# Two buffers instead of one for the rows of a tile that are scattered with gate and token

## The chip, the cores and the metric

The kernel runs on one core of a Trainium2 chip. The metric is the device time of one execution in microseconds (us).

The engines have these short names in the profile: PE is TensorE's matmul, PEld its weight load, DVE is VectorE, ACT is ScalarE, POOL is GpSimd and SP is SyncE, which issues most transfers. A "q" behind a name (SPq) is that engine's instruction queue.

## The reference

Three layers follow each other on 1152 tokens of 512 values.

```python
# attention: 2 batches, 8 heads, 576 positions, 64 values a head; each row keeps its 32 largest scores
scores = scale * q @ k.T
mask = scores >= kth_largest(scores, 32)
attn = softmax(where(mask, scores, -1e9)) @ v            # -> x [1152, 512]
# dense layer, 512 -> 2048 -> 512
h = x @ w_in
x = (h * cos(h)) @ w_out
# mixture of experts, 8 experts of width 1024, one expert per token
probs = softmax(x @ w_gate); e = argmax(x @ w_gate)
slot = place of the token among the tokens of expert e, in token order; kept if slot < 288
out[token] = probs[token, e] * (relu(x[token] @ w1[e]) @ w2[e])
```

## The kernel before

All operations are registered with a planner (`Plan`): engine, an estimated cost, the tiles that are read and written, and a rank. `Plan.emit` then simulates the engines with these costs. At each step it takes, over all engines, the operation that can start first, and among those of one engine that can start within 0.02 us of each other, the one of lowest rank (then the older in the list). So the order of instructions on each engine follows from these simulated times. A tile belongs to a ring with a fixed number of buffers; an operation that opens a new tile of a ring can be chosen only when a buffer is free in the simulation, and on the chip it waits by semaphore until the last user of the buffer is done.

There are 36 attention steps. The tokens form nine tiles of 128. The tiles are handled in groups: tile 0 alone, then the pairs (1, 2), (3, 4), (5, 6) and (7, 8). For each group the dense layer runs as `layer_in` (L662, matmuls L684 to L686), `cosine` (L712), `product` (L720, on GpSimd) and `layer_out` (L729), which sums a tile in the PSUM tile `x2` (two buffers). The matmuls of a pair's two tiles alternate, and those of the second end last.

Then each tile goes through `route` and `place`:

- `route`, L742: ScalarE copies `x2` into `xr`, a buffer of 128 rows of 520 values. L743 (helper line L660): TensorE transposes the rows into `pt` (two buffers). L744: ScalarE copies them to `gT` (one buffer). L748: four matmuls, recorded as eight instructions, give the logits in the PSUM tile `av` (one buffer, which logits and counts share). L751 to L756 (`pick`, VectorE) find the expert; L751 and L752 read `av`. L768: ScalarE takes the exponential. L759 to L761 write the gate into column 512 of `xr`; L764 and L765 (GpSimd) write the token number into column 513 and zeros behind it.
- `place`, L786: TensorE counts the earlier tokens of each expert, into `av`. L789 to L792 (`address`, VectorE) work out the slot of each row; L789 is the last that reads `av`. L795: GpSimd scatters the rows of `xr` to the DRAM tensor `xs` with an indirect transfer.

The buffer `xr` is in use from L742 until the scatter of L795 has landed. Tile 4 uses a buffer of its own, `xr4`, and its `place` comes last, after that of tile 8. The order in the list is route(7), place(7), route(8), place(8), place(4), at one rank for each pair.

When all nine scatters have landed, SyncE gathers the slots of expert 0 (L953, L956); transfers of later weights (L936, L939) stand behind it in the same queue. The experts follow: transposes (L963, L964), first layer (L978, L980), second layer (L1009), scatter to the output (L1015). Their weights are split into a high and a low part on ScalarE (L944) and VectorE (L946).

ScalarE changes its function table (ACT_TABLE_LOAD) whenever the sine of L712 and the exponentials of L561 and L768 alternate.

```python
    ring("x2", "ps", [128, 512], F32, 2)
    ring("av", "ps", [128, 512], F32, 1, tag="av")
    ring("gT", "mx", [128, 512], F32)
    ring("xr", "mx", [128, RW], F32)
    ring("xr4", "mx", [128, RW], F32, tag="raw")
    ...
        kx = ("xr4" if t == 4 else "xr", t)
```

Of the kernel before, what the change touches and what calls it, by code (L numbers as in the profile page):

```python
# [7 lines left out]
F32 = mybir.dt.float32  # L8
# [17 lines left out]
RW = 520  # L26
# [197 lines left out]
@with_exitstack  # L224
def kernel(ctx, tc, kq, vn, vs_, w_in, w_out, w_gate, w1, w2, capacity, out):

    assert int(capacity) == CAP
    ctx.enter_context(tc.manual_schedule())  # L230
    args = (tc, kq, vn, vs_, w_in, w_out, w_gate, w1, w2, out)
    const = ctx.enter_context(tc.tile_pool(name="const", bufs=1, side="left"))
    dram = ctx.enter_context(tc.tile_pool(name="dram", bufs=1, space=DRAM))
    kept = {}

    def lasting(name, shape, dtype, pool=const):
        if name not in kept:
            kept[name] = pool.tile(shape, dtype, name=name)
        return kept[name]
    kept["xs"] = dram.tile([SLOTS, RW], F32, name="xs")  # L240

    flag, more, unproven = forward(lasting, *args, True)
    with tc.If(flag() > 0):
        more()
        with tc.If(unproven() > 0):
            flag, more, _ = forward(lasting, *args, False)
            with tc.If(flag() > 0):
                more()
# [3 lines left out]
def forward(ctx, lasting, tc, kq, vn, vs_, w_in, w_out, w_gate, w1, w2, out, paired):  # L252
# [18 lines left out]
    def ring(name, pool, shape, dtype, bufs=1, tag=None, gate=None):  # L271
        P.ring(name, lambda: pools[pool], shape, dtype, bufs, tag, gate)
# [379 lines left out]
    ring("ur", "mx", [128, 2, 512], F32, 2, tag="ur")  # L652
    ring("nn", "mx", [128, 512], F32)
    ring("gT", "mx", [128, 512], F32)
    ring("xr", "mx", [128, RW], F32)
    ring("xr4", "mx", [128, RW], F32, tag="raw")

    def transposes(kp, src):
# [477 lines left out]
```

## Time and profile before

| | us |
|---|---|
| median of 3 runs | 705.67 (705.2 to 707.3) |
| profiled execution | 706.96 |
| its span (first to last instruction) | 705.1 |
| PE busy | 596.7 (85%) |
| PEld busy | 434.8 (62%) |
| DVE busy | 553.4 (78%) |
| ACT busy | 496.0 (70%) |
| POOL busy | 265.2 (38%) |

The share of busy time is a mean over stages that have different limits, so it doesn't tell by itself which engine bounds the kernel. All times within the span are counted from its first instruction. The granted clock of TensorE is given as a share of full speed: 1.00 is 2.4 GHz, 0.50 is 1.2 GHz, and a value between them is a stretch that has both.

### The profile page before, as it was taken

How to read it: one execution, taken by the hardware profiler on the slowest of the kernel's cores; microseconds unless marked ns; L12 is line 12 of the kernel's file. 1: busy time of each engine (PE TensorE's matmuls, PEld its weight loads, DVE VectorE, ACT ScalarE, POOL GpSimd, SP SyncE). 2: the span in 40 equal slices, each digit the busy share in tenths (PEclk: the TensorE clock that was granted, in tenths of full speed). 3: DMA queues.
4: the chain of work that ended last, by engine and by line, in shares of the span. 5: the costliest groups of instructions: out<-in, count | busy, mean ns of one | idle time of the engine just before them, and what ended most of it. 6: DMA issues, size and time to landing. Idle time of an engine off the chain costs nothing.

```text
span 705.1 us, 11071 instructions
## 1 busy us (share of the span) xinstructions
PE 596.7 (85%) x3611; PEld 434.8 (62%) x3611; DVE 553.4 (78%) x1654; ACT 496.0 (70%) x1004; POOL 265.2 (38%) x316
## 2 busy tenths in 40 slices
PE   3333576898999999989999899999639999999994
PEld 1122355645776655866665676666328888888893
DVE  5999999999999899999999953566115777779630
ACT  4666998999799988778877764476015777777630
POOL 3366675677345544554544432223110110011111
PEclk9999868999899999999999999999857999999998
DMA  8543552064221201100000003444023777778200
GB/s 330 198 150 122 164 163 91 1 236 172 67 89 39 76 0 38 35 1 17 1 1 1 1 17 119 140 144 150 31 78 119 230 241 223 226 257 254 71 17 16
DMA packets 29635, 76.24 MB, mean 108 GB/s; under 512 B 3966, under 2 KB 3966, under 8 KB 29568
## 3 DMA queue, kind: packets, MB, share of 16 engines
q1 hardware_dynamic: 27824, 70.68, 30.3%
q0 software_dynamic: 1744, 4.76, 1.8%
q8 instruction: 30, 0.49, 0.3%
q14 instruction: 37, 0.30, 0.2%
HBM read 63.52 MB, written 12.69 MB: 108 GB/s over the span
## 4 chain that ended last, share of the span: by engine, by line
PE 41%; DVE 34%; ACT 16%; DMA 3%; issue 3%; POOL 1%; SPq 1%; POOLq 0%; DVEq 0%; ACTq 0%
PE yp L1009 11%; DVE W L513 9%; DVE C L517 8%; PE hp L978 7%; PE x L729 7%; DVE C L509 4%; PE hp L980 3%; ACT Sp L561 2%; ACT pen L556 2%; DVE W L522 2%; DVE wt L405 2%; ACT Sp L570 2%; ACT Sp L494 2%; PE h L684 2%; DVE Sp L574 2%
## 5 line engine op out<-in xcount | busy, mean ns | idle before, releaser
L729 PE MATMUL x<-wo,hs 128*128 128x512 f32 x288 | 138.2, 603 | 0.0
L946 DVE TENSOR_TENSOR wl<-raw,wh 128x512 fp32r<-128x512 f32 x128 | 90.4, 741 | 41.9 <-ACT wh L944 38.7
L559 POOL TENSOR_TENSOR Sp<-Sp,pen 128x576 f32<-128x576 f32 x72 | 97.5, 1354 | 64.8 <-ACT pen L556 64.5
L513 DVE MAX8 W<-C 128x8 f32<-128x288 f32 x288 | 118.2, 446 | 0.6
L517 DVE MATCH_REPLACE8 C<-W,C 128x288 f32<-128x288 f32 x216 | 93.8, 440 | 0.0
L589 PE MATMUL pt<-ident,Sp 128*128 128x128 f32 x324 | 56.4, 304 | 38.6 <-ACT Sp L570 31.6
L482 PE MATMUL S<-kq 64*128 64x288 f32 x256 | 58.4, 539 | 30.8 <-ACT Sp L494 20.9
L944 ACT ACTIVATE wh<-raw 128x512 fp32r<-128x512 f32 x128 | 74.5, 622 | 9.9 <-DMA raw<-in_w_dram 6.9
L589 PEld LDWEIGHTS pt<-ident,Sp 128*128 128x128 f32 x324 | 40.4, 154 | 66.1 <-ACT Sp L570 41.0
L684 PE MATMUL h<-xh,wh 128*128 128x256 f32 x256 | 78.0, 305 | 0.5 <-ACT hs L691 0.4
L1015 POOL DMA_INDIRECT out_dram<-ot,ti x16 | 17.9, 1117 | 159.0 <-ACT ot L1024 124.8
L978 PE MATMUL hp<-xgs,wh 128*128 128x384 f32 x256 | 76.9, 370 | 0.0
L729 PEld LDWEIGHTS x<-wo,hs 128*128 128x128 f32 x288 | 49.0, 190 | 43.4 <-issue 42.7
L685 PE MATMUL h<-xl,wh 128*128 128x256 f32 x256 | 71.9, 281 | 0.0
L686 PE MATMUL h<-xh,wl 128*128 128x256 f32 x256 | 71.8, 281 | 0.0
L1009 PE MATMUL yp<-wh,hc 128*128 128x512 f32 x192 | 70.1, 405 | 0.0
L509 DVE TENSOR_TENSOR C<-Sp 128x576 f32<-128x576 f32 x72 | 64.5, 896 | 3.7 <-ACT Sp L494 2.9
L720 POOL TENSOR_TENSOR hs<-hs,ur 128x512 f32<-128x512 f32 x36 | 48.4, 1353 | 46.5 <-ACT ur L712 45.1
L980 PE MATMUL hp<-xgs,wl 128*128 128x192 f32 x256 | 65.5, 256 | 0.0
L561 ACT ACTIVATE Sp<-Sp,tb 128x576 f32<-128x576 f32 x72 | 55.7, 774 | 13.1 <-POOL Sp L559 12.9
L556 ACT ACTIVATE pen<-Sp,tb 128x576 bf16<-128x576 f32 x72 | 55.3, 768 | 6.3 <-POOL tb L549 5.5
L591 ACT ACTIVATE PT<-pt 128x384 f32<-128x384 f32 x108 | 48.5, 483 | 12.1 <-PE pt L589 12.0
(138 smaller groups left out, 1371.8 us busy)
## 6 DMA issues: line engine op xcount, KB each, us to landing
raw<-in_w_dram SPq DMA_DIRECT2D x64, 512.0 KB, 3.9
wraw<-in_w_out_dram SPq DMA_DIRECT2D x16, 512.0 KB, 3.9
wraw<-in_w_in_dram SPq DMA_DIRECT2D x16, 512.0 KB, 3.9
xs<-z SPq DMA_DIRECT2D x1, 4680.0 KB, 16.0
kq<-in_kq_dram SPq DMA_DIRECT2D x8, 576.0 KB, 7.8
v<-in_vn_dram SPq DMA_DIRECT2D x8, 320.0 KB, 5.5
v<-in_vs_dram SPq DMA_DIRECT2D x8, 320.0 KB, 3.0
out_dram<-z SPq DMA_DIRECT2D x1, 2304.0 KB, 21.0
```

Source lines behind the costliest of these rows:

```text
L509: DVE.tensor_tensor(out=T["C", s], in0=x[:, :, 0:HS], in1=x[:, :, HS:S], op=op)
L513: P.op("dve", 0.365, lambda r=r, i=i: DVE.max(T["W", s][:, i, LIST[r]:LIST[r] + 8], T["C", s][:, i, :]), r=[("C", s, i)], w=[("W", s, i)])
L517: P.op("dve", 0.42, lambda r=r, i=i: DVE.match_replace(T["C", s][:, i, :], T["W", s][:, i, LIST[r]:LIST[r] + 8], T["C", s][:, i, :], NEG), ...
L559: P.op("pool", 1.34, lambda i=i, kp=kp: POOL.tensor_tensor(out=T["Sp", s][:, i, :], in0=T["Sp", s][:, i, :], in1=T[kp], op=OP.subtract), r ...
L589: PE.transpose(T[kp][:, c * 128:(c + 1) * 128], P2[:, cc * 128:(cc + 1) * 128], ident)
L684: PE.matmul(o, hi, a, start=(kc == 0), stop=False, skip_group_check=True)
L729: P.op("pe", 0.86, lambda f=f, a=a: PE.matmul(T["x2", t], T[kh][:, a:a + 128], T["wo", 0][:, f, :], start=(f == 0), stop=(f == 15)), r=[kh ...
L944: P.op("act", 0.52, lambda a=a, hi=hi: ACT.activation(T[hi], T[kr][:, a * 512:(a + 1) * 512], AF.Copy), r=[kr], w=[hi])
L946: P.op("dve", 0.6, lambda a=a, hi=hi, lo=lo: DVE.tensor_tensor(out=T[lo], in0=T[kr][:, a * 512:(a + 1) * 512], in1=T[hi], op=OP.subtract), ...
L978: PE.matmul(T[kp][:, 0:2 * MAIN], T[ka][:, c:c + 128], x.rearrange("p a n -> p (a n)"), start=(kc == 0), stop=False, skip_group_check=True)
L980: PE.matmul(T[kp][:, 0:MAIN], T[kb][:, c:c + 128], x[:, 0], start=False, stop=(kc == 3), skip_group_check=True)
L1009: PE.matmul(T[kp], x, w, start=(fc + n == 0), stop=(fc == 7 and n == len(uses) - 1))
```

## The change

The ring `xr` gets two buffers. That is 2,080 bytes more in each partition of the pool `mx`. The planner's simulation counts with two buffers as well.

```diff
     ring("nn", "mx", [128, 512], F32)
     ring("gT", "mx", [128, 512], F32)
-    ring("xr", "mx", [128, RW], F32)
+    ring("xr", "mx", [128, RW], F32, 2)
     ring("xr4", "mx", [128, RW], F32, tag="raw")
```

## Rows read from the trace of the kernel before

**Rows 1.** Stretches: us, busy us (instructions) by engine, clock, DMA share, GB/s.
```profile
283.00:415.00 132.00, 124.91 (x891) 90.00 (x889) 127.28 (x421) 100.00 (x192) 64.63 (x84) 1.00 0.03 10
415.00:503.00 88.00, 87.98 (x455) 57.03 (x452) 38.93 (x84) 48.16 (x85) 22.42 (x23) 1.00 0.35 114
503.00:527.00 24.00, 6.68 (x61) 5.42 (x59) 4.66 (x36) 2.58 (x7) 3.21 (x5) 0.58 0.16 51
...
538.00:690.00 152.00, 151.97 (x839) 131.76 (x839) 110.70 (x323) 105.30 (x262) 15.99 (x14) 1.00 0.57 183
```

**Rows 2.** Line L742, idle time ahead of it by releaser: us, times.
```profile
  DMA xs<-xr,slot: 4.8, 1
```

**Rows 3.** Order of time, 501 to 521 us: start, duration, engine, line, operation.
```profile
501.76 0.60 ACT L742 ACTIVATE xr<-x 128x512 f32<-128x512 f32 x1 [8.08 <-PE x L729]
...
503.14 0.60 PE L660 MATMUL pt<-ident,xr 128*128 128x128 f32 x4
...
503.84 0.60 ACT L744 ACTIVATE gT<-pt 128x512 f32<-128x512 f32 x1 [1.48 <-PE pt L660]
...
504.49 1.06 PE L748 MATMUL av<-wg,gT 128*128 128x8 f32 x8 [0.75 <-ACT gT L744]
...
505.68 0.15 DVE L752 COPY small<-av 128x8 f32<-128x8 f32 x1
...
507.52 0.08 DVE L789 DVE_READ_ACCUMULATOR small<-av,onehot 128x1 f32 x1
...
507.84 0.27 DVE L792 TENSOR_SCALAR slot<-small 128x1 int32<-128x1 f32 x1
508.90 1.04 POOL L795 DMA_INDIRECT xs<-xr,slot  x1 [14.01 <-DVE slot L792]
511.81 0.60 ACT L742 ACTIVATE xr<-x 128x512 f32<-128x512 f32 x1 [4.78 <-DMA xs<-xr,slot]
...
512.47 1.12 PE L660 MATMUL pt<-ident,xr 128*128 128x128 f32 x4 [5.33 <-ACT xr L742]
...
514.33 1.87 PE L748 MATMUL av<-wg,gT 128*128 128x8 f32 x8 [0.75 <-ACT gT L744]
...
517.26 0.17 PE L786 MATMUL av<-onehot,tri 128*128 128x8 bf16 x1 [1.06 <-DVE small L756]
...
519.56 0.99 POOL L795 DMA_INDIRECT xs<-xr,slot  x1 [7.51 <-DVE small L815]
```

**Rows 4.** The chain of waits: start, duration, what stands in it.
```profile
496.33 6.97 PE x L729 x16
...
508.90 2.81 DMA xs<-xr,slot
```

**Rows 5.** SyncE's queue at the first gather, in order of time.
```profile
523.84 0.33 SPq L953 DMA_DIRECT2D xg<-xs  x1
...
527.17 1.06 SPq L936 DMA_DIRECT2D raw<-in_w_dram  x2
```

**Rows 6.** Short stretches, columns as in rows 1, for the clock.
```profile
506.00:507.00 1.00, 0.39 (x8) 0.35 (x7) 0.54 (x4) 0.36 (x2) 0.00 (x0) 0.87 0.00 0
507.00:508.00 1.00, 0.14 (x2) 0.05 (x2) 0.77 (x7) 0.04 (x1) 0.00 (x0) 0.50 0.00 0
...
537.00:538.00 1.00, 1.00 (x8) 1.00 (x7) 0.43 (x2) 0.30 (x2) 0.00 (x0) 0.77 0.00 0
```

**Rows 7.** Order of time, tiles 5 and 6: a scatter and the next copy.
```profile
464.45 1.06 POOL L795 DMA_INDIRECT xs<-xr,slot  x1 [10.28 <-DVE ur L695]
...
469.25 0.60 ACT L742 ACTIVATE xr<-x 128x512 f32<-128x512 f32 x1 [1.49 <-POOL hs L720]
```

**Rows 8.** Order of time on ScalarE around one load of a function table.
```profile
459.78 1.15 ACT L944 ACTIVATE wh<-raw 128x512 fp32r<-128x512 f32 x2 [0.54 <-DMA raw<-in_w_dram]
460.95 1.28 ACT L768 ACT_TABLE_LOAD   x1
462.25 0.30 ACT L768 ACTIVATE small<-small 128x8 f32<-128x8 f32 x1
```

## The prediction

> **What bounds the kernel now.** I read the table of stretches first. From 283 to 415 us VectorE is busy 127.28 of 132 us [rows 1]; that is the attention. From 415 to 503 us TensorE is busy 87.98 of 88 us, and from 538 to 690 us 151.97 of 152 [rows 1]: the dense layers and the experts. Between these two lies a hole: in the 24 us from 503 to 527 no engine is busy more than 6.7 us, and TensorE's granted clock averages 0.58 [rows 1]. Nothing is saturated there; something is a chain of waits. So I went to the tile that the change doubles, `xr`, and to the order of time in the hole.
>
> The list of what ended the idle time ahead of the copies into `xr` has the scatter out of `xr` once, with 4.8 us of ScalarE's time [rows 2]. Nine tiles go through `route`, so eight rounds show no such wait. The order of time shows where it is: the last pair of tiles, 7 and 8 [rows 3]. Tile 7 goes copy (501.76), transposes (503.14), copy to `gT` (503.84), logits (504.49), pick, count, address (slot at 507.84 + 0.27), scatter (508.90). Only at 511.81, when that scatter has landed, does tile 8 begin with the same copy; then transposes at 512.47, logits at 514.33, and its scatter at 519.56; tile 4's, from a buffer of its own, follows it. SyncE, stopped behind them, issues the first gather at 523.84 [rows 5]. The chain of waits agrees: the scatter of tile 7 stands in it for 2.81 us, directly ahead of tile 8's copy [rows 4]. Tile 8's sums were ready long before, when the run of sixteen matmul instructions ended at 496.33 + 6.97 = 503.30 [rows 4]. The experts cannot start before the gather, and from there to the end TensorE has no gap. So what is saved before 523.84 is saved at the end of the kernel.
>
> **The change part by part.** No instruction is added or taken away; 2,080 bytes per partition more are reserved. What goes is one wait: tile 8's copy no longer waits for tile 7's scatter. The order in which instructions are issued comes from the planner's simulated times, in which `xr` is free sooner, so the order may change too.
>
> What is late next? I rebuild the end with the durations of [rows 3].
>
> - Tile 8's copy. Tile 7's sums end two matmuls ahead, at 503.30 − 4 × 6.97/16 = 501.56, and its copy starts at 501.76, 0.20 later. So tile 8's can start at 503.50 and ends, after 0.60, at 504.10, instead of 511.81 + 0.60 = 512.41.
> - Collision. ScalarE also wants to copy `gT` of tile 7 at 503.84. One must wait: with tile 8's copy first, `gT` runs 504.10 to 504.70 and tile 7 is 0.26 us later than now.
> - TensorE. Tile 8's transposes fit before tile 7's logits (504.16 to 504.76), as `pt` has two buffers. Tile 7's logits run 504.76 to 505.82, now 504.49 + 1.06 = 505.55: 0.27 late.
> - The next resources. `gT` has one buffer and the PSUM tile `av` has one, and both logits and counts of both tiles use `av`. `gT` is free at 505.82, so tile 8's second copy ends by 506.45. `av` is the later one: pick 7 reads it, then count 7 fills it, and address 7 reads it last at 507.52 + 0.08, that is 507.87 after the 0.27 shift. From the end of what it waits for to TensorE's start it is some 0.06 us (tile 8's copy ended at 512.41, its transposes began at 512.47). Tile 8's logits start at about 507.93.
> - From there nothing is new. From tile 8's logits to the gather it is 523.84 − 514.33 = 9.51 us now, with the same instructions. The gather goes out at 507.93 + 9.51 = 517.44.
>
> Saved: 514.33 − 507.93 = **6.4 us**. The wait of 4.8 us is not the size of the gain: what counts is that the whole round of tile 8, up to its logits, moves under the round of tile 7.
>
> Bounds. The most: the planner may put tile 8's logits before tile 7's count, since pick reads `av` only in its first two instructions (L752 at 505.68 + 0.15). Logits 8 then start at about 506.5, pick 8 ends near 508.6, count and address of 7 add about 1.1 us, and from count 8 it is 519.56 − 517.26 = 2.3 us to the scatter: 511.4 to 512.0 instead of 519.56, some 7.6 to 8.2 us. The least: ScalarE or TensorE takes up tile 8 only when tile 7's address is done (508.11); then 511.81 − 508.11 = 3.7 us. I take 6.4, since each engine there is mostly idle and count 7 has the older place in the planner's list, which decides between operations that can start at one time.
>
> Behind the hole all moves as a block: the weight loads that follow stand behind the gather in SyncE's queue (gather 523.84, next loads 527.17) [rows 5], so their distance to expert 0 stays. The slow start of the experts also stays: the clock, at 0.50 in the hole, is back at 1.00 only after about 537.5 (0.77 in that slice) [rows 6], with expert 0 at work, and that moves with the gather.
>
> Ahead of the hole the second buffer gives nothing to the path. Tile 6's copy (469.25) stood behind tile 5's scatter (464.45) [rows 7], but TensorE is full there anyway [rows 1] and hides the delay. If that cover were gone, tile 6 could start up to 469.25 − 464.45 = 4.8 us sooner, the most that is hidden there. A new issue order costs or gives something here, since VectorE's few gaps (132.00 − 127.28 = 4.7 us from 283 to 415) can close or widen: I allow 1.5 us either way, a third of them, as an estimate.
>
> Its own time: the profiled execution took 706.96, of which 705.1 are the span. 706.96 − 6.4 = 700.6; the median of the runs shown is 1.29 lower, so **699.3**.
>
> **Rivals.**
>
> *The clock stays up.* The clock fell between 506 and 508 us (0.87, then 0.50), after TensorE had turned from full work to short pieces [rows 6]. With tile 8's transposes and logits moved into 504 to 509 there is more work there. If these run at 2.4 GHz, transposes take 0.60 for 1.12 and logits 1.06 for 1.87 [rows 3]: at most 1.3 us more, 698.0. Against it: the new work is about 1.7 us spread over five.
>
> *Logits ahead of the count*: 8.2 us, 697.5, as above.
>
> *Late start.* The wait goes over to another single buffer or to a queue in front of tile 8's copy or transposes: 3.7 us, 702.0. For it: `gT` and `av` stay single. Against it: those two bind only after 505.8.
>
> *The order of the attention gets worse.* This is the one on the other side. From tile 2 on, `route` is issued at other places, and its exponential can fall between the sines of the dense layer. ScalarE then loads function tables more often: a load takes 1.28 us, and the next instruction starts 0.02 us behind it [rows 8]. Each needless change to exponential and back is 2.57 us of ScalarE; if the selection on VectorE or a matmul waits for it, it is on the path. Two such pairs on the path (5.1 us) would leave 705.67 − 6.4 + 5.1 = 704.4, three (7.7) would make it 707.0, both within 0.3%, and four (10.3) 709.6. So it decides from the second pair on, and makes the kernel slower from the fourth. Against it: ScalarE is busy 100.00 of 132.00 us from 283 to 415 [rows 1], so a load mostly falls into slack. The Trainium skill (ScalarE: Activation LUTs, "What ACT_TABLE_LOAD costs") puts a drain of 1.38 us beside each load, 2.66 in all. By that, as an estimate, a pair would be 5.3 us, and two of them would already give 705.67 − 6.4 + 10.6 = 709.9; the trace doesn't agree, as the work before the load at 460.95 ended at 460.93, and the work behind it began at 462.25 [rows 8].
>
> **How the numbers follow.** Forecast (6.4 saved, the attention within 1.5): 0.60, own range 697.8 to 700.8. Logits ahead 0.10, clock up 0.10, late start 0.07: all faster. Worse order 0.13, of which 0.08 end within 0.3% (2.1 us, about what a measurement of this kernel can tell) and 0.05 beyond. Faster 0.87, same 0.08, slower 0.05. The range goes from 696.2 (8.2 us and 1.3 of the 1.5 in the attention) to 703.2 (late start and 1.2 lost), and leaves out some 0.15.
>
> **What would show it.** Right: tile 8's copy starts within 1 us after tile 7's sums are copied and before tile 7's scatter; the wait on the scatter is gone from the list of `xr`; tile 8's logits stand right behind tile 7's address; the first gather is some 6.4 us closer to the end of the last layer matmul (now 523.84 − 503.30 = 20.5; then about 14.1); from the gather to the end stays at 181.3. Wrong: the last matmul of the dense layers ends more than 2 us from 503.30, with a different number of table loads ahead of it; or tile 8's copy still starts after tile 7's scatter; or the clock rises later after the gather than now and expert 0 is slower.

## The result, and the profile after

The changed kernel takes 700.31 us (median of 6 runs, 698.24 to 701.6), the kernel before 706.41 (median of 6, 705.2 to 707.85). The ratio is 0.991, with a 95% interval of 0.9892 to 0.9929: 6.1 us faster, where 6.4 were forecast. The forecast time of 699.3 stood against a median before of 705.67. By the interval the gain is 5.0 to 7.6 us.

The profiled execution took 698.34 us (span 696.5). The order of time in the hole, as in [rows 3]:

```profile
494.43 7.11 PE L729 MATMUL x<-wo,hs 128*128 128x512 f32 x16
499.86 0.60 ACT L742 ACTIVATE xr<-x 128x512 f32<-128x512 f32 x1 [8.22 <-PE x L729]
...
501.58 0.60 ACT L742 ACTIVATE xr<-x 128x512 f32<-128x512 f32 x1 [1.12 <-PE x L729]
502.07 0.59 ACT L744 ACTIVATE gT<-pt 128x512 f32<-128x512 f32 x1
...
502.71 1.06 PE L748 MATMUL av<-wg,gT 128*128 128x8 f32 x8 [0.74 <-ACT gT L744]
...
503.63 0.63 PE L660 MATMUL pt<-ident,xr 128*128 128x128 f32 x4
...
505.69 0.08 DVE L789 DVE_READ_ACCUMULATOR small<-av,onehot 128x1 f32 x1
...
505.91 1.03 PE L748 MATMUL av<-wg,gT 128*128 128x8 f32 x8 [0.58 <-DVE small L789]
...
507.06 1.04 POOL L795 DMA_INDIRECT xs<-xr,slot  x1 [14.05 <-DVE slot L792]
...
510.33 0.97 POOL L795 DMA_INDIRECT xs<-xr,slot  x1 [2.23 <-DVE small L815]
...
514.62 0.33 SPq L953 DMA_DIRECT2D xg<-xs  x1
```

Tile 8's copy (501.58) now starts as soon as its sums are there, and it is over before tile 7's scatter is even issued (507.06). What tile 8's logits (505.91) wait for is no longer a scatter but VectorE's last read of `av` (L789): the bracket names it. The list of what ended the idle time ahead of the copies into `xr`, which had the scatter with 4.8 us [rows 2], has one entry left:

```profile
  PE x L729: 10.9, 4
```

The table puts the two traces side by side. The last layer matmul ends, by the chain of waits, at 503.30 before [rows 4] and at 501.56 after (the copy behind it starts at 501.58).

| us | before | after | difference |
|---|---|---|---|
| start to the end of the last layer matmul | 503.30 | 501.56 | −1.74 |
| from there to the start of tile 8's logits | 11.03 | 4.35 | −6.68 |
| from there to the first gather | 9.51 | 8.71 | −0.80 |
| from the gather to the end of the span | 181.26 | 181.88 | +0.62 |
| span | 705.1 | 696.5 | −8.6 |

So the hole itself gives 6.68 + 0.80 = 7.48 us. The 1.74 ahead of it is not the change: 1.39 of it is there already when tile 0 is copied (169.26, before 170.65), and up to tile 5 both kernels issue the same instructions in the same order. The +0.62 behind the gather isn't put down to the change either: the same stretch takes 182.30 us in a second trace of the changed kernel and 181.28 in the first experiment below.

The 0.80 comes from the clock: it is in tile 8's logits, which took 1.03 us instead of 1.87. Short stretches after (columns as in [rows 1]) show where it fell, and where it came back:

```profile
506.00:507.00 1.00, 0.94 (x8) 0.87 (x9) 0.29 (x2) 0.00 (x0) 0.00 (x0) 1.00 0.00 0
507.00:508.00 1.00, 0.00 (x0) 0.00 (x0) 0.90 (x7) 0.00 (x0) 0.94 (x1) 0.88 0.00 0
508.00:509.00 1.00, 0.57 (x9) 0.47 (x9) 0.48 (x7) 0.39 (x2) 0.10 (x1) 0.50 0.35 137
...
528.00:529.00 1.00, 1.00 (x7) 1.00 (x7) 0.41 (x2) 0.29 (x2) 0.00 (x0) 0.88 0.00 0
529.00:530.00 1.00, 1.00 (x9) 1.00 (x9) 0.76 (x2) 1.00 (x4) 0.00 (x0) 1.00 0.00 0
```

Tile 8's logits were done (505.91 + 1.03 = 506.94) before the clock fell (0.88 in the slice from 507). Its return, about 13.6 us behind the gather (528.2 − 514.6), is as late as before (537.5 − 523.8 = 13.7).

### The profile page after: what moved, and what is told of

Its sections match the earlier page's. It is cut to its first block, busy times and chain, and to the rows that moved or that the text cites. A ratio compares the mean times of both kernels' runs of the same rounds, so it can differ in the third digit from the quotient of the medians.

```text
span 696.5 us, 11067 instructions
## 1 busy us (share of the span) xinstructions
PE 593.9 (85%) x3611; PEld 432.4 (62%) x3611; DVE 550.8 (79%) x1654; ACT 496.0 (71%) x1004; POOL 267.1 (38%) x316
## 4 chain that ended last, share of the span: by engine, by line
PE 41%; DVE 35%; ACT 15%; issue 3%; DMA 3%; POOL 1%; SPq 1%; POOLq 0%; DVEq 0%; ACTq 0%
PE yp L1009 11%; DVE W L513 9%; DVE C L517 8%; PE hp L978 8%; PE x L729 7%; DVE C L509 5%; PE hp L980 3%; ACT Sp L561 2%; DVE W L522 2%; ACT pen L556 2%; DVE wt L405 2%; ACT Sp L570 2%; ACT Sp L494 2%; PE h L684 2%; DVE wt L403 2%
## 5 line engine op out<-in xcount | busy, mean ns | idle before, releaser
L559 POOL TENSOR_TENSOR Sp<-Sp,pen 128x576 f32<-128x576 f32 x72 | 98.9, 1373 | 63.6 <-ACT pen L556 63.0
L946 DVE TENSOR_TENSOR wl<-raw,wh 128x512 fp32r<-128x512 f32 x128 | 88.4, 725 | 40.0 <-ACT wh L944 39.1
L1009 PE MATMUL yp<-wh,hc 128*128 128x512 f32 x192 | 70.0, 405 | 0.0
L561 ACT ACTIVATE Sp<-Sp,tb 128x576 f32<-128x576 f32 x72 | 55.7, 773 | 14.5 <-POOL Sp L559 14.2
```

The source lines that it names most:

```text
L559: P.op("pool", 1.34, lambda i=i, kp=kp: POOL.tensor_tensor(out=T["Sp", s][:, i, :], in0=T["Sp", s][:, i, :], in1=T[kp], op=OP.subtract), r ...
L946: P.op("dve", 0.6, lambda a=a, hi=hi, lo=lo: DVE.tensor_tensor(out=T[lo], in0=T[kr][:, a * 512:(a + 1) * 512], in1=T[hi], op=OP.subtract), ...
L1009: PE.matmul(T[kp], x, w, start=(fc + n == 0), stop=(fc == 7 and n == len(uses) - 1))
```

## The experiments

Two theories stood against each other. The first is that of the prediction: all is gained in the hole. The rival: the planner, counting with two buffers, issues things in another order from tile 6 on, and that gives the time. On TensorE the order differs first behind tile 5's count: tile 6's transposes now stand ahead of the next 24 matmuls of `layer_in`, behind which they stood before.

**A buffer for tile 8 alone.**

```diff
-    ring("xr", "mx", [128, RW], F32)
+    ring("xr", "mx", [128, RW], F32); ring("xr8", "mx", [128, RW], F32)
...
-        kx = ("xr4" if t == 4 else "xr", t)
+        kx = ("xr4" if t == 4 else "xr8" if t == 8 else "xr", t)
```

The second line stands so in `route` and in `place`; the same holds for the next experiment.

> Only tile 8 gets a buffer of its own; tiles 0 to 3 and 5 to 7 still share one, and the issue order differs from that of the kernel before at one place, the transposes of tile 8. Theory (the gain is made in the hole alone, where tile 8's round moves under tile 7's): the stretch from the last layer matmul to the first gather falls from 20.5 us to about 13.1, as with two buffers for all, and the time is 5 to 7.5 us below before. Rival (the gain comes from the new issue order from tile 6 on): the time stays within 0.3% of before and so does the stretch.

Measured: 698.92 us, before 705.78 on that chip; ratio 0.9898 (0.9872 to 0.9924). In order of time, tile 8's copy, its logits and the gather:

```profile
502.29 0.60 ACT L742 ACTIVATE xr<-x 128x512 f32<-128x512 f32 x1 [0.98 <-PE x L729]
...
506.69 1.03 PE L748 MATMUL av<-wg,gT 128*128 128x8 f32 x8 [0.64 <-DVE small L789]
...
515.39 0.33 SPq L953 DMA_DIRECT2D xg<-xs  x1
```

The sums end at 502.26, so from there to the gather it is 13.13 us, after 13.06 in the changed kernel. Against the kernel before, only tile 8's own operations change place in the order, on TensorE, ScalarE and GpSimd. So with the order of tiles 0 to 7 left as it was, the whole gain is there. The theory holds.

**Two buffers, but one for the last pair.**

```diff
-    ring("xr", "mx", [128, RW], F32)
+    ring("xr", "mx", [128, RW], F32); ring("xrB", "mx", [128, RW], F32)
...
-        kx = ("xr4" if t == 4 else "xr", t)
+        kx = ("xr4" if t == 4 else "xrB" if t in (1, 3, 6) else "xr", t)
```

> Two buffers with fixed users: tiles 1, 3 and 6 have one, tiles 0, 2, 5, 7 and 8 the other. So all pairs but the last are free of the wait, and the issue order up to tile 7 is that of the changed kernel. Theory (the hole alone): the stretch from the last layer matmul to the first gather is 20.5 us as before, and the time is within 0.3% of before. Rival (issue order, or the waits of the earlier tiles): 6 us below before.

Measured: 705.97 us (12 runs), before 705.78; ratio 0.9995 (0.9978 to 1.0013). Tile 6's copy and tile 8's copy and logits, in order of time:

```profile
460.10 0.58 ACT L742 ACTIVATE xrB<-x 128x512 f32<-128x512 f32 x1
...
509.70 0.60 ACT L742 ACTIVATE xr<-x 128x512 f32<-128x512 f32 x1 [4.73 <-DMA xs<-xr,slot]
...
512.22 1.88 PE L748 MATMUL av<-wg,gT 128*128 128x8 f32 x8 [0.74 <-ACT gT L744]
```

Tile 6's copy comes 9.2 us earlier than in [rows 7] (460.10 for 469.25; tile 5's copy came 2.3 us earlier, 453.95 for 456.24), and nothing comes of it. Tile 8 waits as before, and from the last sum (494.33 + 6.97 = 501.30) to the gather (521.74) it is 20.44 us, before 20.54. So the rival falls: neither the earlier waits nor the order gives anything that can be measured.

**The next limit: tile 8's logits out of `av`.** The logits of tile 8 go to the PSUM tile that held its transposes.

```diff
-        kp, kg, kl = ("pt", ("r", t)), ("gT", ("r", t)), ("av", ("r", t))
+        kp, kg, kl = ("pt", ("r", t)), ("gT", ("r", t)), ("pt" if t == 8 else "av", ("r", t))
```

> The changed kernel, with the logits of tile 8 in the PSUM tile that held its transposes instead of in av. Theory (after the change, av is what tile 8 waits for next): its logits start right behind the count of tile 7, some 3.7 us after the last layer matmul instead of 4.3, and the first gather 12.5 us after that matmul instead of 13.1; in the time 0.6 us, too little for the comparison of times. Rival (VectorE or gT is what comes next): the gather stays at 13.1 us.

Measured: 700.01 us, ratio 0.99 (0.9875 to 0.9926), not to be told from the changed kernel. Tile 8's copy, logits and scatter, and the gather:

```profile
504.09 0.60 ACT L742 ACTIVATE xr<-x 128x512 f32<-128x512 f32 x1 [1.12 <-PE x L729]
...
507.74 1.85 PE L748 MATMUL pt<-wg,gT 128*128 128x8 f32 x8
...
512.89 0.97 POOL L795 DMA_INDIRECT xs<-xr,slot  x1 [2.27 <-DVE small L815]
...
517.16 0.33 SPq L953 DMA_DIRECT2D xg<-xs  x1
```

The logits start 3.67 us after the sums (507.74 − 504.07), no longer 4.35, and there is no wait on L789 ahead of them: the limit was `av`, and 0.7 us are saved at that place. But the clock had fallen by then (0.50 from about 507.3), the logits took 1.85 us, and the gather goes out 13.09 us after the sums, as without the edit. Against an execution of the changed kernel whose logits took 1.85 as well (the last one below: 13.79) it is 0.7 us sooner. Inconclusive in the time, clear in the trace.

**TensorE kept at work in the hole.** 2, 3 and 24 matmuls are added; the code of the last 24:

```diff
+    spin = lambda n, name, i: n and P.op("pe", 0.22 * n, lambda: [PE.matmul(T["h", ("spin", name)][:, 0:128], ident, ident, ...) for _ in range(n)], ...)
...
-        P.op("pe", 0.1, count, ...)
+        spin(24, "c", P.op("pe", 0.1, count, ...))
```

> The changed kernel, with 29 matmuls of 128x128 values added whose result nobody reads: 2 behind the count of tile 7, 3 behind the logits of tile 8, and 24 behind the last count, while the scatters and the gather run. Theory (expert 0 starts slowly only because the clock fell in the hole): if the clock is back at 1.00 when expert 0 begins, its first layer, now 6 us at 0.50, takes half, and the kernel is about 3 us faster than the changed one. Rivals: the clock falls again while the transposes wait for the gather, and nothing is gained; or the added matmuls run at 0.50 for their whole length (about 10 us), still stand in the queue when the gather lands, and cost up to 4 us.

Measured: 701.53 us, ratio 0.9936 (0.9913 to 0.9959), not faster than the changed kernel (0.991, 0.9892 to 0.9929); whether it is slower stays open, as the intervals overlap. The clock by stretches, then tile 8's logits in order of time, then a row of the chain of waits:

```profile
506.00:515.00 9.00, 8.47 (x62) 8.25 (x61) 3.84 (x29) 0.39 (x2) 2.98 (x3) 0.50 0.18 67
516.00:519.00 3.00, 3.00 (x30) 3.00 (x28) 0.00 (x0) 0.00 (x0) 0.00 (x0) 1.00 0.02 6
519.00:522.50 3.50, 1.30 (x7) 0.62 (x5) 0.29 (x2) 0.48 (x2) 0.00 (x0) 1.00 0.75 226
523.00:529.50 6.50, 5.14 (x19) 4.42 (x18) 1.65 (x7) 1.36 (x4) 0.00 (x0) 0.50 0.42 160
```

```profile
506.94 1.72 PE L748 MATMUL av<-wg,gT 128*128 128x8 f32 x8
```

```profile
512.05 5.86 DMA xs<-xr,slot x2
```

The first rival came true. The added work brought the clock back at 516, but TensorE then waited for the gather (1.30 us of work in 3.50) and it fell again before expert 0's first layer. Besides, the matmuls put ahead held tile 8 up: its logits begin at 506.94, 4.67 us after the sums (502.27), in the changed kernel 4.35. And in this execution the last scatter landed 4.6 us after its issue instead of 2.8 (513.33 to 517.91); why stays open, since the next run, with the same 24 matmuls, doesn't show it. From the gather to expert 0's second layer (L1009 at 537.66 in the chain) it is 19.51 us, 1.1 less than in the changed kernel's first trace (20.61), so what this run loses, it loses ahead of the gather.

**At work through the gather.** The 24 stay, the five ahead go, and 2, 3 and 6 stand behind the first three pairs of transposes of expert 0:

```diff
-            P.op("pe", 0.4, tr, r=[kx], w=[kp], duty=0.5)
+            spin((e == 0) * (2, 3, 6, 0)[c], ("hp", (0, "spin")), P.op("pe", 0.4, tr, r=[kx], w=[kp], duty=0.5))
```

> The changed kernel with 24 added matmuls of 128x128 values behind the last count, as in the run before, none ahead of it, and 2, 3 and 6 more behind the first three pairs of transposes of expert 0, where TensorE waits for the gather; nobody reads them. Theory (expert 0 is slow only because the clock is at 0.50): the clock is back at 1.00 before the gather lands, stays there, and the first layer of expert 0 takes 3 us less; the gather is issued 13.1 us after the last layer matmul as in the changed kernel, and the time is 2 to 3 us below that kernel's. Rivals: the added matmuls between the transposes hold these up by as much as the clock gives (no change in time); or the last scatter lands late again (4.6 us instead of 2.8) because of the added work, which costs 1.8 us.

> The changed kernel on the chip of the run beside it, for the comparison: some 6 us below before; last layer matmul to first gather 13.1 to 13.9 us, the upper end where the clock has fallen before tile 8's logits.

Measured on one chip, before 705.79: this 697.66 us, ratio 0.9891 (0.987 to 0.9912); the changed kernel 700.15, ratio 0.9923 (0.9902 to 0.9944). Stretches of this kernel, then of the changed one:

```profile
510.00:514.00 4.00, 4.00 (x25) 4.00 (x23) 0.70 (x5) 0.00 (x0) 1.94 (x2) 0.50 0.35 133
...
515.00:518.00 3.00, 2.83 (x26) 2.63 (x24) 0.00 (x0) 0.00 (x0) 0.00 (x0) 1.00 0.56 143
518.00:522.80 4.80, 4.34 (x30) 3.54 (x30) 1.22 (x5) 0.99 (x3) 0.00 (x0) 1.00 0.79 281
522.80:528.00 5.20, 5.20 (x36) 5.13 (x37) 2.50 (x9) 2.77 (x9) 0.00 (x0) 1.00 0.05 19
```

```profile
505.00:506.00 1.00, 0.43 (x8) 0.24 (x6) 0.68 (x5) 0.72 (x3) 0.00 (x0) 0.82 0.00 0
506.00:509.00 3.00, 2.14 (x12) 1.99 (x12) 1.12 (x10) 0.18 (x2) 1.01 (x1) 0.50 0.00 0
518.00:524.40 6.40, 3.00 (x9) 1.46 (x9) 1.18 (x5) 0.99 (x3) 0.00 (x0) 0.50 0.75 257
524.40:529.50 5.10, 5.10 (x20) 5.10 (x20) 1.28 (x5) 1.36 (x4) 0.00 (x0) 0.50 0.05 19
```

From the gather to expert 0's second layer (first L1009 in the chain) it is 533.14 − 514.63 = 18.51 us with the clock kept up, 536.99 − 516.26 = 20.73 in the changed kernel beside it, and 535.23 − 514.62 = 20.61 in its first trace. In its first stretch of about 5 us expert 0 gets through 36 matmuls instead of 20. So 2.1 to 2.2 us are saved from the gather on, less than the 3 expected. From the last transposes (L963) to the second layer it is 10.67 us instead of 13.72 and 13.30: there the clock gives 2.6 to 3.1, as expected. What is missing lies ahead of these transposes, which begin 7.84 us after the gather instead of 6.89 and 7.43. In order of time, VectorE's first instruction behind the last transfer of the gather, and the transposes:

```profile
521.68 0.17 DVE L958 CAST ti<-xg 128x2 int32<-128x2 f32 x1 [1.83 <-DMA xg<-xs]
...
522.47 0.27 PE L963 MATMUL xp<-ident,xg 128*128 128x128 f32 x1
```

The added matmuls directly ahead are only a part of that: from that instruction to the transposes it is 0.79 us instead of 0.48 and 0.49, so they hold them up by 0.3. The instruction itself, which waits for the transfer, starts 7.05 us after the gather was issued, in the changed kernel's traces 6.41 and 6.94: 0.64 and 0.11 of the delay are the transfer. Why it differs so much stays open.

This version has the lowest median of all, 2.5 us below the changed kernel on that chip. The buffer for tile 8 alone (698.92 us, ratio 0.9898) ran on another chip, and the two can't be told apart by these runs. A kernel with the 24 matmuls alone wasn't run, so what the eleven between the transposes give by themselves isn't shown.

The hole in the traces (us from the end of the last layer matmul):

| kernel | tile 8's logits start | they take | first gather |
|---|---|---|---|
| before | 11.03 | 1.87 | 20.54 |
| two buffers, one for the last pair | 10.92 | 1.88 | 20.44 |
| changed | 4.35 | 1.03 | 13.06 |
| changed, again | 4.37 | 1.85 | 13.79 |
| buffer for tile 8 alone | 4.43 | 1.03 | 13.13 |
| logits of tile 8 apart | 3.67 | 1.85 | 13.09 |
| TensorE kept at work | 4.67 | 1.72 | 15.88 |
| at work through the gather | 4.37 | 1.03 | 13.06 |

## Why the prediction was right, point by point

The likeliest case came, with a bit of a rival in it. That 6.1 us came so close to 6.4 is in part luck: the hole gave 7.48 us in the first trace of the changed kernel and 6.75 in the second (20.54 − 13.79), and the interval of the measured gain reaches from 5.0 to 7.6.

- *The size.* The round of tile 8 was to start its logits 6.4 us sooner, at 4.63 us after the sums; it starts them 6.68 sooner, at 4.35. That the 4.8 us of the wait isn't the size of the gain is shown: 6.68 and 7.48 are both above it.
- *The collision on ScalarE* was priced at 0.26 us and didn't take place. Tile 8's copy begins 0.02 us after the sums by the trace, not 0.20, and `gT` of tile 7 begins at 502.07 while that copy is recorded until 502.18. From the sums to `gT` it is 0.51 us, before 0.54. These 0.26 are nearly all of the 0.28 by which the logits come sooner than forecast.
- *TensorE.* I put tile 8's transposes ahead of tile 7's logits; they stand behind them (503.63). I had looked at `pt` alone. In the code `transposes` is registered as writing `gT` as well (`w=[kp, kg]`), and `gT` has one buffer, so the planner can't choose tile 8's transposes before tile 7's logits have read it. It makes no difference, since `av` is what tile 8 waits for, as forecast: the wait on L789 stands in the row, and it goes away in the experiment that takes the logits out of `av`.
- *From the logits to the gather* I counted 9.51 us. It is 8.71 in the first trace and 9.42 in the second of the changed kernel. The rival of the clock, priced at 1.3 us at most, gives 0.8 where it occurs: the transposes are off the path, the logits are on it. Of the traces with a shortened hole and no work added ahead of them, three have the logits at 1.00 and two at 0.50, so which of the two a run gets was not forecast.
- *Behind the hole* all moved nearly as a block: 181.26 us before, 181.88 and 182.30 in the two traces of the changed kernel, and the clock comes back as late after the gather as before. "From there to the end TensorE has no gap" was wrong: in the kernel before it was busy 15.93 of the 20.66 us from 523.84 to 544.50, and 6.04 of the last 15.10. The conclusion doesn't need it, since what stands behind the gather waits for it.
- *Ahead of the hole* nothing was gained, as forecast, and the second experiment shows it by itself. But "from tile 2 on, `route` is issued at other places" was wrong: the order differs from tile 6 on only, so the attention, which I let vary by 1.5 us and in which the rival on the other side was placed, is the same in both kernels. The table loads on ScalarE are as many as before (15, 11 and 3 at L712, L561 and L768). That rival could not come about, and its 0.13 was too much: it hung on an order that the planner's simulated times fix, and I had not followed these up to tile 6.

## What to carry to other kernels

In this kernel a single buffer on a serial chain cost not the wait that the profile shows at it (4.8 us), but the whole of the next round that could run under the present one, up to the next shared buffer (6.7 us): look for that buffer, and count to it. The same wait occurred in several places; only the one where no engine was full was worth anything, and a table of stretches told which that was. TensorE's idle time ahead of the experts was paid again in their first stretch, at half clock, with 2.6 to 3.1 us. Work that nobody reads was cheaper, but only when it went on until the real work started and little waited behind it.

## What was not expected of the hardware

In two traces of the changed kernel, with the same instructions in the same order, the clock fell 6.2 us after the last layer matmul (at 507.8, sums at 501.56) and 3.2 us after it (at 505.6, sums at 502.47). What decides between the two stays open here; it moves the gather by 0.7 us (13.06 and 13.79 us behind the sums), through one matmul group.
